# Values by 64x64 quarters, scores moved to the top of the tile, and conversions spread over three tiles

## The chip, the cores and the metric

One core of a Trainium2 chip runs one program. TensorE multiplies matrices from SBUF into PSUM, which has eight banks of 512 float32 columns on 128 partitions. VectorE (DVE), ScalarE (ACT) and GpSimd (POOL) work on the results, and SyncE (SP) issues nearly all DMAs. Each engine works through its own queue in order. The metric is the device time of one execution in microseconds (us). Before the change it is 1263.37 us, the median of three executions (1262.73 to 1265.43).

## The reference, cut to what matters

Attention inside chunks of 64 tokens (8 batches, 8 heads of 64 columns, 576 tokens each), then two feed-forward layers over all 4608 tokens:

```python
scores = scale * q_c @ k_c.T;  scores -= max(scores)      # per chunk of 64 tokens
attn = exp(scores) / (sum(exp(scores)) + 1e-9)
x = attn @ v_c                                            # heads side by side: 512 columns
h = x @ w_in                                              # 512 -> 1024
solu = h * softmax(h);  ln = (solu - mean) / sqrt(var + 1e-6) * g_ln
y = ln @ w_out                                            # 1024 -> 512
h2 = y @ w_in2                                            # 512 -> 2048
out = maximum(0.01 * h2, h2) @ w_out2                     # 2048 -> 512
```

Everything is float32 at the interface. The weights come as 64-bit words and are converted to float32 on the chip ("pieces" of 512 columns).

## The kernel before, in words

The first part of the program, about 550 us, takes the tokens in 36 tiles of 128: two chunks of 64 in every tile, eight heads in four pairs. For a tile it does, over several turns of the loop `for t in range(1, T + 2)`: scores (`qk_mm`), maxima, subtraction and exponentials (`softmax_a`), sums and division (`softmax_b`), transposition (`pt_mm`, `pt_copy`), values (`pv_mm`), splitting of the result into a high and a low part (`x_split`: `x_hi` on ACT, `x_lo` on DVE), the first layer in two halves of 512 columns (`ff1_mm(t, 0)` and `ff1_mm(t, 1)`, twelve matmuls each), softmax and normalisation (`solu_*`), transposition (`lnT_mm`, `lnT_split`), and, from tile 5 on, one group of the second matrix a turn (`y1_group`, 24 matmuls). The second part, the last 710 us, is the second feed-forward layer as a chain of matmuls (`h2_product`, `out_product`); the change does not touch it, except that its PSUM pool is opened later under another name.

The order on every engine is written out by hand: it is the order of the calls in the loop. In turn t the scores are those of a later tile: tile t + 2 at the top of the turn while t <= AHEAD = 5, and from t = 5 on tile t + 3, inside `attend(t)`, straight behind the values of tile t + 1. Two kinds of turn matter. In most, `y1_group` stands between `pt_mm(t + 1)` and `attend(t)`. In a "late" turn (t = 5, 9, 13, ... 33) `attend(t)` comes earlier, before `ff1_mm(t, 1)`, and `y1_group` stands at the end of the turn. "Tile t" below also means turn t.

Values before: V lies in `vbd` as block-diagonal operands with zeros, so that one matmul has 128 partitions of keys (two heads) and 64 output columns; 16 such matmuls make a tile. Their result lies in one bank, `ptx`, which `pt_mm` uses too; the scores have two banks, `s0` and `s1`. In tile 1 the scores are in the `ef` banks.

Conversion of a piece: ACT takes magnitudes (`take_magnitudes`, L101), DVE clamps and shifts (`convert_a`, L108 and L110) and joins the bits (`convert_b`, L114 and L118), POOL and ACT finish it. In turns 2, 3 and 5 all of this stands at the end of the turn, in later ones between `softmax_b` and the end.

Of the kernel before, what the change touches and what calls it, by code (L numbers as in the profile page):

```python
# [17 lines left out]
P = 128  # L18
# [34 lines left out]
def kernel(  # L53
# [18 lines left out]
    ps1 = ctx.enter_context(tc.tile_pool(name="ps1", bufs=1, space=bass.MemoryType.PSUM))  # L72

    ps2 = ws = yp = None

    def bank(tag, name):
        return (ps2 if tag == "ef" else ps1).tile([P, 512], F32, tag=tag, name=name)

# [227 lines left out]
    with tc.manual_schedule():  # L306

        with ExitStack() as phase:
            ps2 = phase.enter_context(
# [10 lines left out]
            vbd = [pa.tile([P, KD, 2, 2, D], F32, tag=f"vbd{i}", bufs=1, name=f"vbd{i}") for i in range(2)]  # L320
# [18 lines left out]
            def qk_mm(t):  # L339
                ps = s_ps[t] = [  # L340
                    bank("ef" if t == 1 else f"s{e}", "s_ps").rearrange("p (h n) -> p h n", h=H)[:, :KD]
                    for e in range(2)
                ]
# [12 lines left out]

            def softmax_a(t):
# [53 lines left out]
            def x_hi(t):  # L411
                x = xs[t] = pa.tile([P, 2, KD, P], F32R, tag="xs", name="xs")
                act.activation(x[:, 0], x_ps[t], AF.Copy)  # L413

            def x_lo(t):
                ps, x = x_ps.pop(t), xs[t]
                dve.tensor_tensor(x[:, 1], ps, x[:, 0].bitcast(F32), op=ALU.subtract)
# [82 lines left out]
            def lnT_mm(t):  # L500
                u = us.pop(t)
                for hf in range(2):
                    tag = ("s0", "ptx")[hf] if t == T - 2 else "ef"
                    ps = ln_ps[t, hf] = bank(tag, "ln_ps").rearrange("p (i n) -> p i n", i=4)
# [19 lines left out]
            def y1_group(b, m):  # L524
                pairs = (slice(0, 2), slice(0, 3, 2), slice(1, 3))[b % 3]
                bnk = bank("s1" if (b, m) == (NB - 1, 0) else "ef", "y_ps")
# [50 lines left out]
            for i, eng in enumerate((dve, pool)):  # L577
                eng.memset(vbd[i][0:D, :, :, 1], 0.0)
                eng.memset(vbd[i][D:P, :, :, 0], 0.0)
# [20 lines left out]
            def exponentials(t):  # L600
                ps, sm = s_ps.pop(t), st8[t]
                for h in range(H):
                    act.activation(
                        es[t][:, h],
                        ps[h % 2][:, h // 2],
# [6 lines left out]
            def maxima(t):  # L612
                sm = st8[t] = pa.tile([P, 2, H], F32, tag="st8", name="st8")
                es[t] = pa.tile([P, H, D], F32, tag="es", name="es")
                for i in range(2):
                    dve.reduce_max(sm[:, 0, i::2], s_ps[t][i], axis=AX)
# [104 lines left out]
            for t in range(1, T + 2):  # L721
# [12 lines left out]
                if t <= AHEAD:  # L734
                    load_qk(t + 3)
# [13 lines left out]
                pieces = 0 if t in (1, 4) or t >= T - 2 else 2 if t in DOUBLE else 1  # L749
                if 0 < t <= AHEAD:  # L750
# [6 lines left out]
                if t <= AHEAD:  # L757
# [24 lines left out]
                if 1 < t < T:  # L782
                    solu_max(t, 0)
                if 1 <= t <= T:
# [22 lines left out]
                else:  # L807
# [28 lines left out]

        wb = ctx.enter_context(tc.tile_pool(name="wb", bufs=1, reuse_waits="tile"))
# [290 lines left out]
```

## Time and profile before

| | before |
|---|---|
| median of 3 executions | 1263.37 us |
| the profiled execution, device time | 1262.47 us |
| its span, first to last instruction | 1260.7 us |
| TensorE busy | 1228.4 us (97%) |
| DVE busy | 897.1 us (71%) |
| ACT busy | 573.3 us (45%) |
| POOL busy | 285.2 us (23%) |
| mean granted TensorE clock | 0.996 of full |

The device time is 1.8 us longer than the span. In a timeline row the first number is the start, the second the time from the first start to the last end of the merged instructions; ends of matmuls are modelled and overlap the next row, so what a step takes on TensorE is best read as the distance from its start to the start of the next row. A bracket at the end of a row is the idle time of the engine before it and what ended that. An fp32 matmul of 64 columns is recorded as two instructions, so a tile's 16 matmuls appear as x32.

### The profile page before, as it was taken

What the parts mean: (1) busy time and instruction counts of PE and PEld (TensorE: products, weight loads), DVE (VectorE), ACT (ScalarE), POOL (GpSimd) and SP (SyncE); (2) the same over time, 40 slices, a digit from 0 to 9 for tenths busy, and PEclk for the clock granted to TensorE, in tenths of its full rate; (3) what the DMA queues carried; (4) which work ended last, traced back from release to release, by engine and by line L of the source; (5) the groups of instructions that cost most, each with busy time, mean ns of one, the idle gap of its engine ahead of it and who ended that gap; (6) DMA issues with size and microseconds to landing.
All of it is one profiled execution on the core that took longest, in us unless ns stands there. A gap on an engine that the chain in (4) does not pass through costs nothing.

```text
span 1260.7 us, 22964 instructions
## 1 busy us (share of the span) xinstructions
PE 1228.4 (97%) x8554; PEld 1092.5 (87%) x8554; DVE 897.1 (71%) x1603; ACT 573.3 (45%) x1078; POOL 285.2 (23%) x390
## 2 busy tenths in 40 slices
PE   5989999999999999999999999999999999999998
PEld 4678888778878887899989988998999899989987
DVE  7888778877886887435786677577657766775674
ACT  6645545555545545433442353344235243442451
POOL 0355656655765666200000000000000000000000
PEclk8999999999999999999999999999999999999999
DMA  7535546645676573549889978988898899789676
GB/s 247 163 96 149 176 151 216 235 161 160 207 210 198 157 224 107 186 170 322 262 293 306 293 242 274 310 269 247 291 309 255 262 297 302 240 260 301 197 221 197
DMA packets 171070, 288.83 MB, mean 229 GB/s; under 512 B 50000, under 2 KB 80720, under 8 KB 169936
## 3 DMA queue, kind: packets, MB, share of 16 engines
q1 hardware_dynamic: 170592, 286.78, 71.4%
q8 instruction: 69, 1.13, 0.4%
q10 hardware_dynamic: 368, 0.59, 0.1%
q14 instruction: 41, 0.34, 0.1%
HBM read 239.08 MB, written 48.23 MB: 228 GB/s over the span
## 4 chain that ended last, share of the span: by engine, by line
PE 85%; DVE 8%; ACT 4%; DMA 1%; issue 1%; SPq 0%; ACTq 0%
PE h_ps L871 28%; PE o_ps L928 19%; PE y_ps L534 13%; PE h_ps L435 10%; PE o_ps L939 10%; PE x_ps L399 2%; PE ln_ps L507 2%; PE s_ps L349 1%; DVE lnT L522 1%; ACT us L458 1%; PE pt_ps L383 1%; DVE us L466 1%; DVE wf L114 1%; DVE wf L118 1%; DVE wf L108 1%
## 5 line engine op out<-in xcount | busy, mean ns | idle before, releaser
L871 PE MATMUL h_ps<-yo,w_s 128*128 128x384 f32 x2016 | 351.0, 334 | 0.0
L871 PEld LDWEIGHTS h_ps<-yo,w_s 128*128 128x128 f32 x2016 | 349.3, 188 | 0.7
L928 PE MATMUL o_ps<-wo_s,yo 128*128 128x512 f32 (+1 forms) x1016 | 262.9, 393 | 0.0
L435 PE MATMUL h_ps<-wi,xs 128*128 128x512 f32 x864 | 211.2, 397 | 1.0 <-ACT xs L413 0.7
L534 PE MATMUL y_ps<-lnT,wo 128*128 128x512 f32 (+1 forms) x888 | 204.2, 386 | 0.0
L928 PEld LDWEIGHTS o_ps<-wo_s,yo 128*128 128x128 f32 x1016 | 179.0, 188 | 28.7
L435 PEld LDWEIGHTS h_ps<-wi,xs 128*128 128x128 f32 x864 | 159.7, 189 | 35.3 <-ACT xs L413 0.8
L534 PEld LDWEIGHTS y_ps<-lnT,wo 128*128 128x128 f32 x888 | 161.7, 188 | 31.9
L939 PEld LDWEIGHTS o_ps<-wo_s,yo 128*128 128x128 f32 x1008 | 144.7, 188 | 15.6
L271 DVE TENSOR_TENSOR yo<-c,yo 128x768 fp32r<-128x768 f32 x144 | 132.4, 951 | 32.0 <-ACT yo L270 30.6
L939 PE MATMUL o_ps<-wo_s,yo 128*128 128x256 f32 x1008 | 149.7, 283 | 0.0
L850 ACT ACTIVATE c<-h_c 128x384 f32<-128x384 f32 x144 | 72.9, 526 | 127.4 <-DVE h_c L882 127.4
L882 DVE TENSOR_TENSOR h_u<-h_ps,h_p 128x384 f32<-128x384 f32 x96 | 53.3, 555 | 106.3 <-PE h_ps L871 99.6
L270 ACT ACTIVATE yo<-c 128x768 fp32r<-128x768 f32 x144 | 113.1, 838 | 7.1 <-DVE c L912 5.5
L466 DVE SCALAR_TENSOR_TENSOR us<-h_ps,us 128x512 f32<-128x512 f32 x72 | 48.7, 690 | 35.4 <-ACT us L458 35.3
L373 POOL TENSOR_TENSOR es<-es,st 128x512 f32<-128x512 f32 x33 | 34.6, 1049 | 156.2 <-DVE st L372 100.7
L522 DVE TENSOR_TENSOR lnT<-ln_ps,lnT 128x512 fp32r<-128x512 f32 x72 | 45.8, 679 | 33.7 <-ACT lnT L518 33.7
L458 ACT ACTIVATE us<-h_ps,z 128x512 f32<-128x512 f32 x72 | 48.7, 682 | 40.2 <-DVE z L454 40.2
L270 ACT ACTIVATE yo<-a 128x768 fp32r<-128x768 f32 x36 | 30.0, 840 | 72.6 <-DVE a L265 72.6
L882 DVE TENSOR_TENSOR h_c<-h_ps,h_u 128x384 f32<-128x384 f32 x96 | 53.2, 554 | 12.9 <-PE h_ps L871 12.3
L366 ACT ACTIVATE es<-es 128x512 f32<-128x512 f32 x33 | 20.8, 632 | 89.4 <-DVE es L365 89.4
L399 PEld LDWEIGHTS x_ps<-pt,vbd 128*64 128x64 f32 x1152 | 37.4, 140 | 26.7 <-ACT pt L389 18.4
(90 smaller groups left out, 1426.7 us busy)
## 6 DMA issues: line engine op xcount, KB each, us to landing
w_s<-wi_d SPq DMA_DIRECT2D x336, 256.0 KB, 4.1
wo_s<-wo_d SPq DMA_DIRECT2D x168, 512.0 KB, 4.6
wi_d<-wi SPq DMA_DIRECT2D x8, 1792.0 KB, 6.3
wo_d<-wi SPq DMA_DIRECT2D x8, 1792.0 KB, 7.0
raw<-in_w_out SPq DMA_DIRECT2D x24, 512.0 KB, 5.1
raw<-in_w_in SPq DMA_DIRECT2D x23, 512.0 KB, 5.2
vbd<-in_v SPq DMA_DIRECT2D x72, 128.0 KB, 5.1
a<-y_d SPq DMA_DIRECT2D x24, 384.0 KB, 5.3
```

Of the source, the lines that this page charges most:

```text
L270: act.activation(o[:, 0], x, AF.Copy)
L271: dve.tensor_tensor(o[:, 1], x, o[:, 0].bitcast(F32), op=ALU.subtract)
L399: pe.matmul(ps[e * D : (e + 1) * D, i, c * D : (c + 1) * D], lhsT=vv[:, i, c, e], rhs=pp[:, i, c * D : (c + 1) * D], start=True, stop=True,)
L435: pe.matmul(hs[t, n], lhsT=x[:, a, kk, :], rhs=w[:, b, kk % 2, n, :], start=(kk == 0 and a == 0 and b == 0), stop=(kk == KD - 1 and a == 1),)
L458: act.activation(u[:, c], hs[t, n], AF.Exp, bias=z[:, 0:1], accum_out=z[:, 8 + n : 9 + n])
L466: dve.scalar_tensor_tensor(u[:, c], hs.pop((t, n)), 1.0 / FF1, u[:, c], op0=ALU.mult, op1=ALU.mult, accum_out=z[:, 10 + n : 11 + n],)
L534: pe.matmul(ps[:, part], lhsT=w[:, a, kk % 4, m * P : (m + 1) * P], rhs=lnT[:, c, kk, pairs, :][:, part], start=(kk == 0 and a == 0 and c ...
L850: act.activation(blocks[block, j // 2][:, j % 2], src, AF.Prelu, alpha=0.01)
L871: pe.matmul(ps, lhsT=w[:, a, kk * P : (kk + 1) * P], rhs=y[:, c, kk, :], start=(first and kk == 0 and a == 0 and c == 0), stop=(kk == 1 an ...
L882: dve.tensor_tensor(o, ps, x, op=ALU.add)
L928: pe.matmul(ps[:, : 2 * P * (a.stop - a.start)], lhsT=x[:, 0, kk, m * P : (m + 1) * P], rhs=w[:, kk, a].rearrange("p a n -> p (a n)"), sta ...
L939: pe.matmul(sums[p % 2][m][:, : 2 * P], lhsT=x[:, 1, kk, m * P : (m + 1) * P], rhs=w[:, kk, 0], start=False, stop=(i == PAIRS - 1 and kk = ...
```

## The change

1. Values by quarters: V is loaded without zeros (`vs`, four DMAs for a tile in place of two, in runs of 512 bytes in place of 256), and each matmul has 64 partitions of keys, 64 output columns and 64 columns of probabilities. There are 16 a tile as before. Heads that share the upper or lower partitions write to different banks, so a tile's values need two banks; they are the two of the scores, now one PSUM tile `s`. In tile 1 the values take both `ef` banks, and `x_split` has two instructions on each engine there. The four memsets of zeros at the start go.
2. The subtraction, the maxima and `x_split` go over both banks with one instruction each; the heads lie in another order inside a tile.
3. Scores: `qk_mm(t + 2)` and `softmax_a(t + 2)` stand at the top of the turn in all turns; `attend` keeps the values and their split.
4. In late turns `attend(t)` stands behind `ff1_mm(t, 1)`.
5. First conversions: magnitudes at the end of turns 1 and 2, `convert_a` in the middle of turn 2 and at the end of turn 3, `convert_b` in the middle of turns 3 and 4.

```diff
             def load_v(t):
...
-                for e in range(2):
-                    r = slice(e * D, (e + 1) * D)
-                    sync.dma_start(out=vbd[t % 2][r, :, :, e], in_=v[t, r])
+                for r in range(2):
+                    for e in range(2):
+                        sync.dma_start(
+                            out=vs[t % 2][r * D : (r + 1) * D, 2 * e : 2 * e + 2],
+                            in_=v[t, e * D : (e + 1) * D, r::2],
+                        )
...
             def softmax_a(t):
...
-                for i in range(2):
-                    dve.reduce_max(sm[:, 0, i::2], ps[i], axis=AX)
-                for i in range(2):
-                    m = sm[:, 0, i::2].unsqueeze(2).to_broadcast([P, KD, D])
-                    dve.tensor_tensor(e[:, i::2], ps[i], m, op=ALU.subtract)
+                top = sm[:, 0].rearrange("p (e i) -> p e i", e=2)
+                dve.reduce_max(top, ps, axis=AX)
+                dve.tensor_tensor(
+                    e.rearrange("p (e i) n -> p e i n", e=2),
+                    ps,
+                    top.unsqueeze(3).to_broadcast([P, 2, KD, D]),
+                    op=ALU.subtract,
+                )
...
             def pv_mm(t):
-                ps = x_ps[t] = bank("ptx", "x_ps").rearrange("p (i n) -> p i n", i=KD)
-                vv, pp = vbd[t % 2], pt.pop(t)
-                for i in range(KD):
+                if t == 1:
+                    ps = [bank("ef", "x_ps") for r in range(2)]
+                    ps = [x.rearrange("p (a n) -> p a n", a=KD)[:, :2] for x in ps]
+                    x_ps[t] = [(r, x) for r, x in enumerate(ps)]
+                else:
+                    both = two_banks("x_ps").rearrange("p r (a n) -> p r a n", a=KD)[:, :, :2]
+                    ps = [both[:, r] for r in range(2)]
+                    x_ps[t] = [(slice(0, 2), both)]
+                vv, pp = vs[t % 2], pt.pop(t)
+                for a in range(2):
                     for c in range(2):
-                        for e in range(2):
-                            pe.matmul(
-                                ps[e * D : (e + 1) * D, i, c * D : (c + 1) * D],
-                                lhsT=vv[:, i, c, e],
-                                rhs=pp[:, i, c * D : (c + 1) * D],
-                                start=True,
-                                stop=True,
-                            )
+                        for r in range(2):
+                            k = slice(r * D, (r + 1) * D)
+                            for e in range(2):
+                                pe.matmul(
+                                    ps[r][e * D : (e + 1) * D, a, c * D : (c + 1) * D],
+                                    lhsT=vv[k, 2 * e + a, c],
+                                    rhs=pp[k, 2 * e + a, c * D : (c + 1) * D],
+                                    start=True,
+                                    stop=True,
+                                )
...
             def attend(t):
 
                 pv_mm(t + 1)
-                if AHEAD <= t < T - 3:
-                    qk_mm(t + 3)
-                    load_qk(t + 4)
                 x_split(t + 1)
-                if AHEAD <= t < T - 3:
-                    softmax_a(t + 3)
...
-                if 0 < t <= AHEAD:
+                if t + 2 < T:
                     qk_mm(t + 2)
...
-                if t <= AHEAD:
+                if t + 2 < T:
                     softmax_a(t + 2)
...
+                if t == 2:
+                    convert_a()
+                elif 2 < t < AHEAD:
+                    convert_b(load=False)
+                    owed = 1
...
-                    elif t < T - 1:
+                    elif t < T - 1 and not late:
                         attend(t)
                     if 1 < t < T:
                         ff1_mm(t, 1)
+                    if late and 1 < t < T - 1:
+                        attend(t)
...
-                        take_magnitudes(pieces)
-                        convert_a(pieces)
-                        convert_b(pieces, load=t == AHEAD)
-                        owed = pieces if t < AHEAD else 0
+                        take_magnitudes(pieces if t == AHEAD else t < 3)
+                        convert_a(pieces if t == AHEAD else t == 3)
+                        if t == AHEAD:
+                            convert_b(pieces)
```

TensorE, from the values of tile 7 (`x_ps`) to the transposition of tile 8 (`pt_ps`); `s_ps` are scores, `ln_ps` a transposition, `h_ps` the first layer. Before:

```order
L399 MATMUL x_ps<-pt,vbd_105 64x64 x16
L349 MATMUL s_ps<-kb_103,qt 64x64 x16
L507 MATMUL ln_ps<-ident,us 128x128 x8
L435 MATMUL h_ps<-wi_173,xs 128x512 x4
L435 MATMUL h_ps<-wi_355,xs 128x512 x4
L435 MATMUL h_ps<-wi_173,xs 128x512 x2
L435 MATMUL h_ps<-wi_355,xs 128x512 x2
L435 MATMUL h_ps<-wi_173,xs 128x512 x4
L435 MATMUL h_ps<-wi_355,xs 128x512 x4
L435 MATMUL h_ps<-wi_173,xs 128x512 x2
L435 MATMUL h_ps<-wi_355,xs 128x512 x2
L383 MATMUL pt_ps<-ident,es 128x128 x4
```

And now, at the same place:

```order
L421 MATMUL x_ps<-pt,vs_105 64x64 x16
L535 MATMUL ln_ps<-ident,us 128x128 x8
L460 MATMUL h_ps<-wi_172,xs 128x512 x4
L460 MATMUL h_ps<-wi_353,xs 128x512 x4
L460 MATMUL h_ps<-wi_172,xs 128x512 x2
L460 MATMUL h_ps<-wi_353,xs 128x512 x2
L359 MATMUL s_ps<-kb_103,qt 64x64 x16
L460 MATMUL h_ps<-wi_172,xs 128x512 x4
L460 MATMUL h_ps<-wi_353,xs 128x512 x4
L460 MATMUL h_ps<-wi_172,xs 128x512 x2
L460 MATMUL h_ps<-wi_353,xs 128x512 x2
L396 MATMUL pt_ps<-ident,es 128x128 x4
```

The scores moved from behind the values to between the two halves of the first layer.

DVE, from the maximum of tile 2's first half (L450) to the start of turn 3 (L454); `xs` is `x_lo`, `lnT` the split behind the transposition, `wf` a piece. Before:

```order
L450 TENSOR_REDUCE z<-h_ps 128x1
L417 TENSOR_TENSOR xs<-x_ps,xs 128x512
L522 TENSOR_TENSOR lnT<-ln_ps,lnT 128x4x128 x2
L108 TENSOR_SCALAR wf<-wf 128x512
L110 TENSOR_SCALAR wf<-wf 128x512
L114 SCALAR_TENSOR_TENSOR wf<-raw,wf 128x512
L118 SCALAR_TENSOR_TENSOR wf<-raw,wf 128x512
L450 TENSOR_REDUCE z<-h_ps 128x1
L454 TENSOR_TENSOR z<-z 128x1
```

And now:

```order
L475 TENSOR_REDUCE z<-h_ps 128x1
L110 TENSOR_SCALAR wf<-wf 128x512
L112 TENSOR_SCALAR wf<-wf 128x512
L442 TENSOR_TENSOR xs<-x_ps,xs 128x2x2x128
L550 TENSOR_TENSOR lnT<-ln_ps,lnT 128x4x128 x2
L475 TENSOR_REDUCE z<-h_ps 128x1
L479 TENSOR_TENSOR z<-z 128x1
```

The first two steps of the piece moved ahead of `x_lo`, the other two out of this turn.

TensorE at the start of the program, the first layer of tile 1 behind its values, with what each row waits for. Before:

```order
L399 MATMUL x_ps<-pt,vbd_105 64x64 x14
L435 MATMUL h_ps<-wi_173,xs 128x512 [waits Activation_49]
L435 MATMUL h_ps<-wi_173,xs 128x512 x7
L435 MATMUL h_ps<-wi_173,xs 128x512 [waits DVE_49]
L435 MATMUL h_ps<-wi_173,xs 128x512 x3
```

And now:

```order
L421 MATMUL x_ps<-pt,vs_105 64x64 x12
L460 MATMUL h_ps<-wi_172,xs 128x512 [waits Activation_49]
L460 MATMUL h_ps<-wi_172,xs 128x512 [waits DVE_49]
L460 MATMUL h_ps<-wi_172,xs 128x512 x2
L460 MATMUL h_ps<-wi_172,xs 128x512 [waits Activation_49]
L460 MATMUL h_ps<-wi_172,xs 128x512 x5
L460 MATMUL h_ps<-wi_172,xs 128x512 [waits DVE_49]
```

The wait for DVE that stood at the ninth matmul now stands at the second, because that one writes the `ef` bank that held tile 1's values.

## Rows read from the trace of the kernel before

**Rows 1.** The page: span, TensorE's busy time, the costliest group and its idle time.
```profile
span 1260.7 us, 22964 instructions
PE 1228.4 (97%) x8554; PEld 1092.5 (87%) x8554; DVE 897.1 (71%) x1603; ACT 573.3 (45%) x1078; POOL 285.2 (23%) x390
...
L871 PE MATMUL h_ps<-yo,w_s 128*128 128x384 f32 x2016 | 351.0, 334 | 0.0
```
**Rows 2.** Waits of TensorE: line, what for, us in total, times, longest.
```profile
PE x_ps L399 <- ACT pt L389: 14.0, 12, 3.5
```
**Rows 3.** Timeline of TensorE, tile 14 into tile 15, no waits.
```profile
212.87 1.15 PE L399 MATMUL x_ps<-pt,vbd 128*64 128x64 f32 x32
213.95 0.69 PE L349 MATMUL s_ps<-kb,qt 64*64 64x64 f32 x32
214.58 1.09 PE L507 MATMUL ln_ps<-ident,us 128*128 128x128 f32 x8
215.43 5.74 PE L435 MATMUL h_ps<-wi,xs 128*128 128x512 f32 x24
221.00 0.60 PE L383 MATMUL pt_ps<-ident,es 128*128 128x128 f32 x4
221.36 5.71 PE L534 MATMUL y_ps<-lnT,wo 128*128 128x512 f32 x24
227.00 1.15 PE L399 MATMUL x_ps<-pt,vbd 128*64 128x64 f32 x32
```
**Rows 4.** Timeline of TensorE, tile 2, scores at the top of the turn.
```profile
44.10 3.02 PE L435 MATMUL h_ps<-wi,xs 128*128 128x512 f32 x12
46.95 0.60 PE L383 MATMUL pt_ps<-ident,es 128*128 128x128 f32 x4
...
49.44 3.01 PE L435 MATMUL h_ps<-wi,xs 128*128 128x512 f32 x12
52.38 0.69 PE L349 MATMUL s_ps<-kb,qt 64*64 64x64 f32 x32
```
**Rows 5.** Timeline of TensorE, values in late tile 17 and what follows.
```profile
253.31 1.25 PE L399 MATMUL x_ps<-pt,vbd 128*64 128x64 f32 x32 [2.10 <-ACT pt L389]
...
255.55 3.99 PE L435 MATMUL h_ps<-wi,xs 128*128 128x512 f32 x12
```
**Rows 6.** Stretches: from:to, length, TensorE busy (instructions), granted clock, DMA share, GB/s.
```profile
253.00:259.00 6.00, 5.69 (x75) 0.72 0.02 4
```
**Rows 7.** Timeline of TensorE, values in turns 1, 3 and 4.
```profile
40.80 1.15 PE L399 MATMUL x_ps<-pt,vbd 128*64 128x64 f32 x32 [0.61 <-ACT pt L389]
...
59.01 1.15 PE L399 MATMUL x_ps<-pt,vbd 128*64 128x64 f32 x32 [1.67 <-ACT pt L389]
...
71.53 1.15 PE L399 MATMUL x_ps<-pt,vbd 128*64 128x64 f32 x32 [3.54 <-ACT pt L389]
```
**Rows 8.** Timeline of DVE, end of tile 3: the conversion and the maximum behind it.
```profile
63.79 1.18 DVE L108 TENSOR_SCALAR wf<-wf 128x512 f32<-128x512 f32 x1
...
66.44 0.69 DVE L114 SCALAR_TENSOR_TENSOR wf<-raw,wf 128x512 uint32<-128x512 uint32 x1
...
67.78 0.68 DVE L450 TENSOR_REDUCE z<-h_ps 128x1 f32<-128x512 f32 x1
```
**Rows 9.** Timeline of TensorE, start of the program, first layer of tiles 1 and 0.
```profile
30.15 2.11 PE L435 MATMUL h_ps<-wi,xs 128*128 128x512 f32 x8 [0.69 <-ACT xs L413]
32.53 3.96 PE L435 MATMUL h_ps<-wi,xs 128*128 128x512 f32 x16 [0.27 <-DVE xs L417]
36.42 0.69 PE L349 MATMUL s_ps<-kb,qt 64*64 64x64 f32 x32
```
**Rows 10.** Timeline of DVE: x_lo at the start, in tile 14 and in tile 16.
```profile
31.79 0.68 DVE L417 TENSOR_TENSOR xs<-x_ps,xs 128x512 fp32r<-128x512 f32 x1
...
214.73 0.69 DVE L417 TENSOR_TENSOR xs<-x_ps,xs 128x512 fp32r<-128x512 f32 x1 [1.09 <-ACT xs L413]
...
246.03 0.68 DVE L417 TENSOR_TENSOR xs<-x_ps,xs 128x512 fp32r<-128x512 f32 x1
```

More of the change, by code (lines that the diff above doesn't have):

```diff
@@ L71, with two_banks @@
     dram = ctx.enter_context(tc.tile_pool(name="dram", bufs=1, space=bass.MemoryType.DRAM))
-    ps1 = ctx.enter_context(tc.tile_pool(name="ps1", bufs=1, space=bass.MemoryType.PSUM))
-    ps2 = ws = yp = None
+    ps1 = ps2 = ws = yp = None
     def bank(tag, name):
         return (ps2 if tag == "ef" else ps1).tile([P, 512], F32, tag=tag, name=name)
+    def two_banks(name):
+        return ps1.tile([P, 2, 512], F32, tag="s", name=name)
     ident = const.tile([P, P], F32, name="ident")
@@ L308 @@
         with ExitStack() as phase:
+            ps1 = phase.enter_context(
+                tc.tile_pool(name="ps1", bufs=1, space=bass.MemoryType.PSUM)
+            )
             ps2 = phase.enter_context(
@@ L318 @@
             kbs = [pa.tile([P, KD, 2, D], F32, tag=f"kb{i}", bufs=1, name=f"kb{i}") for i in range(2)]
-            vbd = [pa.tile([P, KD, 2, 2, D], F32, tag=f"vbd{i}", bufs=1, name=f"vbd{i}") for i in range(2)]
+            vs = [pa.tile([P, KD, 2, D], F32, tag=f"vs{i}", bufs=1, name=f"vs{i}") for i in range(2)]
             qt, es, pt, xs, hs, us, st8 = {}, {}, {}, {}, {}, {}, {}
@@ L332, in load_v @@
                     return
-                for e in range(2):
-                    r = slice(e * D, (e + 1) * D)
-                    sync.dma_start(out=vbd[t % 2][r, :, :, e], in_=v[t, r])
+                for r in range(2):
[4 more added lines that the diff above has]
+                        )
             s_ps = {}
             def qk_mm(t):
[L340 to L343, printed above, removed]
+                if t == 1:
+                    ps = [bank("ef", "s_ps") for e in range(2)]
+                    s_ps[t] = ps = [x.rearrange("p (h n) -> p h n", h=H)[:, :KD] for x in ps]
+                else:
+                    both = two_banks("s_ps").rearrange("p e (h n) -> p e h n", h=H)[:, :, :KD]
+                    s_ps[t], ps = both, [both[:, e] for e in range(2)]
                 kb, qq = kbs[t % 2], qt.pop(t)
@@ L412, in x_hi @@
                 x = xs[t] = pa.tile([P, 2, KD, P], F32R, tag="xs", name="xs")
-                act.activation(x[:, 0], x_ps[t], AF.Copy)
+                hi = x[:, 0].rearrange("p (a r) n -> p r a n", a=2)
+                for r, ps in x_ps[t]:
+                    act.activation(hi[:, r], ps, AF.Copy)
             def x_lo(t):
-                ps, x = x_ps.pop(t), xs[t]
-                dve.tensor_tensor(x[:, 1], ps, x[:, 0].bitcast(F32), op=ALU.subtract)
+                hi, lo = (xs[t][:, e].rearrange("p (a r) n -> p r a n", a=2) for e in range(2))
+                for r, ps in x_ps.pop(t):
+                    dve.tensor_tensor(lo[:, r], ps, hi[:, r].bitcast(F32), op=ALU.subtract)
             def ff1_mm(t, half, ks=None):
@@ L502, in lnT_mm @@
                 for hf in range(2):
-                    tag = ("s0", "ptx")[hf] if t == T - 2 else "ef"
-                    ps = ln_ps[t, hf] = bank(tag, "ln_ps").rearrange("p (i n) -> p i n", i=4)
+                    if t == T - 2 and hf == 0:
+                        bnk = two_banks("ln_ps")[:, 0]
+                    else:
+                        bnk = bank("ptx" if t == T - 2 else "ef", "ln_ps")
+                    ps = ln_ps[t, hf] = bnk.rearrange("p (i n) -> p i n", i=4)
                     for i in range(4):
@@ L525, in y1_group @@
                 pairs = (slice(0, 2), slice(0, 3, 2), slice(1, 3))[b % 3]
-                bnk = bank("s1" if (b, m) == (NB - 1, 0) else "ef", "y_ps")
+                bnk = two_banks("y_ps")[:, 1] if (b, m) == (NB - 1, 0) else bank("ef", "y_ps")
                 ps = bnk.rearrange("p (a n) -> p a n", a=2)
@@ L614, in maxima @@
                 es[t] = pa.tile([P, H, D], F32, tag="es", name="es")
-                for i in range(2):
-                    dve.reduce_max(sm[:, 0, i::2], s_ps[t][i], axis=AX)
+                for e in range(2):
+                    ps = s_ps[t][e] if t == 1 else s_ps[t][:, e]
+                    dve.reduce_max(sm[:, 0, e * KD : (e + 1) * KD], ps, axis=AX)
                 dve.tensor_scalar_mul(sm[:, 0, :], sm[:, 0, :], -scale)
@@ L748 @@
                 late = g == 0 or t == T - 1
-                pieces = 0 if t in (1, 4) or t >= T - 2 else 2 if t in DOUBLE else 1
-                if 0 < t <= AHEAD:
+                pieces = 0 if t < AHEAD or t >= T - 2 else 2 if t in DOUBLE else 1
+                if t + 2 < T:
                     qk_mm(t + 2)
@@ L832 @@
                         y1_group(*bm)
+        ps1 = ctx.enter_context(
+            tc.tile_pool(name="ps1b", bufs=1, space=bass.MemoryType.PSUM, reuse_waits="tile")
+        )
         wb = ctx.enter_context(tc.tile_pool(name="wb", bufs=1, reuse_waits="tile"))
```

12 lines of the change are left out of this document (6 added, 6 removed).

## The prediction

> **What bounds the kernel now.** I read the page first, then the waits of TensorE, then its timeline over whole tiles, and DVE's timeline where TensorE waits. TensorE is busy 1228.4 of 1260.7 us, and the costliest group of the second part has no idle time before it [rows 1]. So the second part, which the change leaves alone, gives nothing. In the first part a tile is a chain of TensorE steps each of which begins where the last ends [rows 3]: what a step costs there costs the program that much. The one wait that recurs is that of the values for the copy of the transposed probabilities (`pt_copy`, ACT): 14.0 us in 12 waits [rows 2]. The reader is to see two sources of a gain, shorter steps and these waits, and ask of everything else whether it can push TensorE back.
>
> **The values by quarters.** A tile's values take from 212.87 to 213.95, 1.08 us, the scores behind them to 214.58, 0.63 us [rows 3]. Both are 32 recorded instructions; the scores' are 64x64 with 64 columns, which is the new form of the values, in the same alternation of partitions, columns and banks. So I price the new values at 0.63: 0.45 less a tile. The bounds are 1.08 (a quarter gains nothing) and 0.63; no row has anything shorter.
>
> **The scores' new place.** This is the edit that works against the gain. Before, a turn has values, scores and transposition in a row, then 24 matmuls of the first layer without a break, 215.43 to 221.00, 5.57 us [rows 3]. Now the scores stand between the two halves. Tile 2 shows both halves in that place: the one ahead of scores 2.94 us (49.44 to 52.38), the one behind scores 2.85 us (44.10 to 46.95) [rows 4], 5.79 together, 0.22 more than 5.57. A turn with `y1_group` takes 14.13 us now (212.87 to 227.00) [rows 3]. Afterwards: scores 0.63, first half 2.85, transposition 0.36, `y1_group` 5.64, values 0.63, transposition 0.85, second half 2.94, together 13.90. So 0.23 of the 0.45 is left.
>
> A rule of the Trainium skill speaks here (page TensorEngine Tiling (Array Packing), section Tiling Modes): switching the tiling mode drains TensorE. The trace agrees in direction with the 0.22 us above; by the rule a turn had three switches and now has four, and without a drain the turn would be 13.68 and the sum 1236, which is the first rival below.
>
> Late turns have the same steps and I give them the same 0.23. Turn 5 loses the second of its two score blocks and turn 33 gains one, which cancels. From turn 5 to turn 33 that is 29 x 0.23 = 6.7 us. Turns 1 to 4 have the scores at the top already and keep the whole 0.45: 1.8. Turn 34 computes no scores: 0.45. Sum 8.9 us; I take 8.7, since in turn 1 part of it meets the delay below. Bounds: 0 if a quarter costs 1.08 and the scores' place costs nothing, 15.7 if only the first holds its promise (35 x 0.45); a loss of 6.4 (29 x 0.22) if a quarter gains nothing and the place costs.
>
> **The waits in steady turns.** From turn 6 on nine of the 12 waits, 0.3 to 2.1 us, come to 8.2: the 14.0 of [rows 2] less 0.61, 1.67 and 3.54 in turns 1, 3 and 4 [rows 7]. The largest stand in late turns, where the values come soon after the transposition: 2.10 in turn 17 [rows 5]. There the values now come one half of the first layer later, 2.94 us, which is more than any of these waits. The clock goes with it: behind the wait of turn 17 the granted clock is 0.72 over six microseconds [rows 6], so part of the stretch ran at 1.2 GHz in place of 2.4, and half of the first layer took 3.99 in place of 3.01 [rows 4, 5], 1.0 us more. Together 9.2. A few of the 0.3 us waits may stay: 0.6. Gain 8.6; bounds 4 and 9.2.
>
> What is late next is the scores at the top of a turn, which now must find the shared banks read by `x_lo` of the tile before. In tile 14 `x_lo` begins 0.78 us after the values end by start-to-start (213.95 to 214.73) and lasts 0.69; the second half of the first layer would then still run for over two microseconds. In tile 16, where DVE is behind, it ends at 246.71, hardly before that half does [rows 10]. But DVE's work up to `x_lo` is the same as before: `softmax_a` moved from behind the previous tile's `x_lo` to ahead of this one's. And `x_lo` no longer has ACT's exponential, waiting for DVE, between itself and the split of `lnT`. I count nothing; bound 0.5 in each of the 14 or so turns where DVE is behind, 7 us. Queued behind a waiting score block is all of TensorE's turn, so such a wait would count in full. The values' wait for `softmax_a` has the first half, transposition and `y1_group`, almost 9 us, as cover.
>
> The one-instruction maxima and subtractions save DVE start costs only; DVE is not the bound, so nothing. The two extra DMAs a tile lie on SP, which has a turn's lead for them; nothing.
>
> **The first conversions.** The values of tiles 4 and 5 wait 1.67 and 3.54 us for `pt_copy` [rows 7]; that copy is behind the exponentials of the layer, these behind a maximum on DVE, and that behind a whole conversion, 63.79 to 67.78, 3.99 us in turn 3 [rows 8]. Now turn 2 ends without any of it, so its 1.67 goes. Turn 3 ends with two of the four instructions, which took 2.65 of the 3.99 beside POOL's work (63.79 to 66.44), so at least 1.34 goes, and what goes earlier in the turn goes too: I take 2.2 of 3.54. The other halves stand in mid-turn where DVE waits for ACT; they may hold `x_lo` and with it the scores for 0.3. Gain 3.6; bounds 0 and 5.2.
>
> **The start.** Here the change adds a wait. Before, eight matmuls of tile 1's first layer ran (30.15 to 32.26) while DVE came to `x_lo`; the other 16 began at 32.53 [rows 9]. Now the second matmul writes the bank that held the values and must wait for the first of the two `x_lo` instructions. `x_lo` began at 31.79 and took 0.68 [rows 10]; half of it ends at about 32.2. Then 23 matmuls remain, at 0.24 each (3.89 us by 16), 5.6 us: scores at 37.8 in place of 36.42. Behind this wait are tile 0's layer, its maxima on DVE and ACT's exponentials; `pt_copy` and the values of tile 2 follow them. In turn 1 TensorE waits 0.61 before the values [rows 7], which it had to spare, so I book 0.8 of the 1.4 as a loss; bounds 0 and 1.4. The memsets that go stood in an idle DVE: nothing. Four DMAs for V in place of two push later loads back in SP's queue, with the same bytes in fewer pieces: nothing, bound 1 us either way. At the end of the first part a group of `y1_group` shares banks with a transposition and waits at most for one DVE subtraction, 0.69 [rows 10]: nothing.
>
> **The sum.** 8.7 + 8.6 + 3.6 - 0.8 = 20.1 us. The profiled execution took 1262.5 (its span and 1.8 around it), 0.9 less than the median of 1263.4. 1262.5 - 20.1 = 1242.4; with the median as base 1243.3. I say 1243.
>
> **The rivals.**
> The scores' place is free: the turn keeps all 0.45, 6.4 us more, 1236 to 1237. For it: ends of matmuls are modelled, and the 0.22 compares different turns. Against it: tile 2 shows it on both sides of the scores.
> Shared banks: where DVE is behind, the scores wait for `x_lo`, 7 us as bounded above: 1250. For it: 246.71 in tile 16 is only just in time, and turns get shorter while DVE's work does not. Against it: DVE also loses waits.
> The quarters do not run beside each other as the scores' do and values stay at 1.08: 1243 + 35 x 0.45 = 1259. Against it: the same form runs at 0.63.
> Slower: shared banks in every turn, a mechanism of its own. Values, ACT copy, DVE subtraction and the next scores are now one loop through one pair of banks. If DVE reached `x_lo` so late in all 29 turns that the scores waited over 0.8 us each, 23 us, the gain would be gone; at 1 us each the time is 1272. That needs `x_lo` over 3 us later than in tile 14 in every turn. Beside it stands the skill's rule (the same page, section Performance Considerations) that tiling speeds up TensorE but not the evacuation of PSUM; DVE's 71% [rows 1] does not bear it out here.
>
> **How the numbers follow.** Forecast, 1238 to 1248: 0.60. Place free, 1236: 0.12. Shared banks in some turns, 1250: 0.16. Quarters gain nothing, 1259: 0.05. Slower, 1272: 0.04. Something between that I have not named, about no change: 0.03. The range 1234 to 1253 holds the first three. A measurement of this kernel cannot tell 0.2%, 2.5 us, from no change. Faster by more: 0.93; within: 0.03; slower: 0.04.
>
> **What would show it.** Values of 0.6 to 0.7 us from their start to the next row; scores between two halves of 2.85 to 2.95; a turn of 13.9 us; no wait of the values for `pt_copy` over 0.5 us from turn 6 on, no stretch of clock 0.72; the values of tile 4 without a wait and those of tile 5 with 1 to 1.5; the scores of tile 3 a microsecond later. I would be wrong if `s_ps` shows waits for DVE `xs` of several microseconds in sum, or if values stay over 0.8 us.

## The result, and the profile after

| | before | after |
|---|---|---|
| median (6 executions each, side by side) | 1264.09 us | 1241.94 us |
| lowest to highest | 1262.73 to 1265.43 | 1241.21 to 1242.75 |
| profiled execution | 1262.47 us | 1242.7 us |

The ratio is 0.9825, 95% interval 0.9812 to 0.9837. The forecast was 1243.0 (1234 to 1253). The profiled execution of before is 1.6 us below its median and that of after 0.8 above its own, so the medians lie 22.2 us apart and the spans 19.8. Two lines of the page of after, against [rows 1]: the span, and the busy time of the engines.

```profile
span 1240.9 us, 22946 instructions
...
PE 1218.2 (98%) x8554; PEld 1073.5 (87%) x8554; DVE 892.8 (72%) x1536; ACT 572.0 (46%) x1079; POOL 285.9 (23%) x388
```

TensorE has 10.2 us less work and 9.6 us fewer gaps. Its waits after (line, what for, us in total, times, longest):

```profile
PE x_ps L421 <- ACT pt L402: 2.6, 2, 1.4
PE h_ps L460 <- DVE xs L442: 2.3, 1, 2.3
...
PE s_ps L359 <- DVE xs L442: 1.2, 2, 0.8
```

The values' 14.0 us in 12 waits [rows 2] are 2.6 in two, both in the start: 1.36 at 27.81, which before had too (1.44 at 28.31, listed as `issue` and not among the 14.0), and 1.23 in turn 1, where before had 0.61 [rows 7]. Two waits on `x_lo` (DVE `xs`) are new or larger. TensorE's timeline of after, in order of time: the start, the values in turn 1, the scores behind the values of tile 5, the transposes of turn 7, a steady turn, a late turn, the beginning of the second part.

```profile
31.84 8.36 PE L460 MATMUL h_ps<-wi,xs 128*128 128x512 f32 x23 [2.33 <-DVE xs L442]
40.13 0.69 PE L359 MATMUL s_ps<-kb,qt 64*64 64x64 f32 x32
...
44.03 0.69 PE L421 MATMUL x_ps<-pt,vs 64*64 64x64 f32 x32 [1.23 <-ACT pt L402]
...
73.43 0.69 PE L359 MATMUL s_ps<-kb,qt 64*64 64x64 f32 x32 [0.75 <-DVE xs L442]
...
104.79 0.60 PE L396 MATMUL pt_ps<-ident,es 128*128 128x128 f32 x4
...
208.27 0.69 PE L421 MATMUL x_ps<-pt,vs 64*64 64x64 f32 x32
208.90 1.09 PE L535 MATMUL ln_ps<-ident,us 128*128 128x128 f32 x8
209.75 3.01 PE L460 MATMUL h_ps<-wi,xs 128*128 128x512 f32 x12
212.69 0.69 PE L359 MATMUL s_ps<-kb,qt 64*64 64x64 f32 x32
213.31 3.02 PE L460 MATMUL h_ps<-wi,xs 128*128 128x512 f32 x12
216.17 0.60 PE L396 MATMUL pt_ps<-ident,es 128*128 128x128 f32 x4
...
222.19 0.69 PE L421 MATMUL x_ps<-pt,vs 64*64 64x64 f32 x32
...
244.00 0.60 PE L396 MATMUL pt_ps<-ident,es 128*128 128x128 f32 x4
...
257.95 0.60 PE L396 MATMUL pt_ps<-ident,es 128*128 128x128 f32 x4
...
531.82 58.41 PE L902 MATMUL h_ps<-yo,w_s 128*128 128x384 f32 x336
```

The rows of before that answer to the last four places, from its timeline of TensorE, with the scores of late tile 17 among them:

```profile
107.39 0.60 PE L383 MATMUL pt_ps<-ident,es 128*128 128x128 f32 x4
...
249.59 0.60 PE L383 MATMUL pt_ps<-ident,es 128*128 128x128 f32 x4
...
254.49 1.13 PE L349 MATMUL s_ps<-kb,qt 64*64 64x64 f32 x32
...
267.61 0.60 PE L383 MATMUL pt_ps<-ident,es 128*128 128x128 f32 x4
...
551.54 48.70 PE L871 MATMUL h_ps<-yo,w_s 128*128 128x384 f32 x280
```

Values take 0.63 us (208.27 to 208.90) against 1.08 [rows 3], a steady turn 13.92 (208.27 to 222.19) against 14.13, the late turn of tile 17 13.95 (244.00 to 257.95) against 18.02 (249.59 to 267.61). From turn 7's transposes to the second part it is 427.03 us against 444.15, 17.1 less. Up to turn 7 only 2.6 were gained, because the scores of tile 3 begin 3.7 us later, 40.13 against 36.42 [rows 9]; from those scores to turn 7 it is 64.66 against 70.97, 6.3 less. Together 19.7, as the spans say (19.8).

### The profile page after: what moved, and what is told of

It is laid out like the page before. It is cut to its first block, busy times and chain, and to the rows that moved or that the text cites. A ratio compares the mean times of both kernels' runs of the same rounds, so it can differ in the third digit from the quotient of the medians.

```text
span 1240.9 us, 22946 instructions
## 1 busy us (share of the span) xinstructions
PE 1218.2 (98%) x8554; PEld 1073.5 (87%) x8554; DVE 892.8 (72%) x1536; ACT 572.0 (46%) x1079; POOL 285.9 (23%) x388
## 4 chain that ended last, share of the span: by engine, by line
PE 94%; DVE 4%; ACT 1%; DMA 0%; POOL 0%; issue 0%; POOLq 0%
PE h_ps L902 28%; PE o_ps L959 19%; PE y_ps L562 16%; PE h_ps L460 15%; PE o_ps L970 10%; PE ln_ps L535 2%; PE x_ps L421 2%; PE s_ps L359 1%; PE pt_ps L396 1%; DVE wf L116 1%; DVE wf L120 0%; DVE us L491 0%; DVE z L475 0%; DMA raw<-in_w_in 0%; DVE wf L112 0%; DVE wf L110 0%
## 5 line engine op out<-in xcount | busy, mean ns | idle before, releaser
L460 PE MATMUL h_ps<-wi,xs 128*128 128x512 f32 x864 | 219.9, 404 | 3.5 <-DVE xs L442 2.3
L475 DVE TENSOR_REDUCE z<-h_ps 128x1 f32<-128x512 f32 x72 | 48.9, 681 | 19.7 <-PE h_ps L460 19.6
L570 ACT ACTIVATE ys<-y_ps 128x512 f32<-128x512 f32 x36 | 21.4, 593 | 87.6 <-PE y_ps L562 86.5
L881 ACT ACTIVATE c<-h_ps 128x384 f32<-128x384 f32 x48 | 23.6, 492 | 76.2 <-PE h_ps L902 76.2
```

The lines of the kernel that those rows point to most:

```text
L460: pe.matmul(hs[t, n], lhsT=x[:, a, kk, :], rhs=w[:, b, kk % 2, n, :], start=(kk == 0 and a == 0 and b == 0), stop=(kk == KD - 1 and a == 1),)
L475: dve.reduce_max(sol[t][:, 8 + n : 9 + n], hs[t, n], axis=AX, negate=True)
L881: act.activation(blocks[block, j // 2][:, j % 2], src, AF.Prelu, alpha=0.01)
```

## The experiments

All times are medians of four or five executions; intervals are of the ratio to the kernel before on the same chip. "After" is 1241.94 throughout. The first four experiments share a chip, the others ran on three more. The median of before beside them lies between 1264.1 and 1265.3 us, so a difference between kernels of different chips is good to about 1 us.

### The banks of the start

```diff
-    ps = [bank("ef", "x_ps") for r in range(2)]
+    ps = [bank(tag, "x_ps") for tag in ("ef", "ptx")]
```

> The values of tile 1 go to one bank of ef and to ptx, in place of two banks of ef, so that the second matmul of ff1 of tile 1 finds a bank that held no values. Theory A (the wait for x_lo at the start, and the clock that falls with it, is the term that the prediction booked too small): the wait of 2.33 us at 31.84 goes, ff1 of tile 1 starts some 2 us earlier and runs at the full clock, scores of tile 3 at 36.5 to 37.5 in place of 40.13, and the time falls by 2.5 to 3.5 us against the changed kernel, to 1238.5 to 1239.5. Theory B (the start is hidden by a transfer, the keys and queries of tile 3, or given back within turns 2 to 5): scores of tile 3 move, but the time stays within 0.7 us of 1241.9.

1239.03 us, 0.980 (0.9786 to 0.9813): 2.9 less than after. Its timeline at the same place:

```profile
29.08 2.11 PE L460 MATMUL h_ps<-wi,xs 128*128 128x512 f32 x8 [0.42 <-ACT xs L437]
...
35.76 0.69 PE L359 MATMUL s_ps<-kb,qt 64*64 64x64 f32 x32
```

Eight matmuls run ahead of `x_lo` again, as in [rows 9], and the scores come 4.4 us earlier. The spans differ by 3.8 (1237.1 against 1240.9), the medians by 2.9. Theory A holds; nothing hides the start. This is the fastest kernel of the study.

### Work ahead of the wait

```diff
     high(7)
+    warm(24)
     ff1_mm(1, 0)
```

> 24 transposes of the identity into a spare bank stand ahead of the first ff1 of tile 1: the wait for x_lo stays where it is, TensorE only has work in front of it. Theory A1 (most of the 3.7 us is the granted clock, which falls to 0.50 from 32 to 36 us): the clock stays near 1 from 32 to 41, scores of tile 3 come 2 to 3 us earlier, and the time falls by 2 to 3 us. Theory A2 (the wait itself is the loss, 2.3 us of idle engine): the clock may be better, but scores of tile 3 come at most 1 us earlier and the time stays within 1 us of 1241.9; the transposes could even add a part of their 24 x 0.06 = 1.4 us.

1239.96 us, 0.9807 (0.9794 to 0.9820): 2.0 less. Its timeline, and then the stretch of the clock (from:to, length, TensorE busy, granted clock, DMA share, GB/s), ahead of that of after:

```profile
28.41 2.84 PE L655 MATMUL spare<-ident 128*128 128x128 f32 x24
31.40 5.92 PE L460 MATMUL h_ps<-wi,xs 128*128 128x512 f32 x24
37.25 0.69 PE L359 MATMUL s_ps<-kb,qt 64*64 64x64 f32 x32
```
```profile
32.00:36.00 4.00, 4.00 (x18) 1.00 0.70 211
```
```profile
29.00:32.00 3.00, 0.66 (x2) 0.86 0.28 79
32.00:36.00 4.00, 4.00 (x10) 0.50 0.87 265
```

The first layer still cannot pass `x_lo`: its 24 matmuls start at 31.40, and of those of after one stands ahead of the wait and 23 start at 31.84. But they run at the full clock, and the scores come at 37.25, which is 0.8 us behind before. So of the 3.7 us that the profiled execution of after loses at this place the wait is 0.8 and the lower clock 2.9: in after TensorE was busy 0.66 us in three, and then 1.2 GHz (0.50 of full) was granted for the whole of the next four. By the medians the transposes, 0.12 us each where 0.06 was expected, give back 2.0. The Trainium skill (page TensorE: Matmul & The Clock Gate, Part 1) says that the granted clock follows how busy the engine has been; this pair of runs agrees.

### The values as they were

```diff
...
+                both = bank("ptx", "x_ps").rearrange("p (a r n) -> p r a n", a=2, r=2)
...
-                                    lhsT=vv[k, 2 * e + a, c],
-                                    rhs=pp[k, 2 * e + a, c * D : (c + 1) * D],
+                                    lhsT=vv[:, 2 * e + a, c, r],
+                                    rhs=pp[:, 2 * e + a, c * D : (c + 1) * D],
...
```

The values lie in bank `ptx` again, which the scores do not share, and the memsets of zeros are back.

> The changed kernel's order with the values as they were: 128 partitions deep with half of the weights zero, 32 matmuls of 64 columns one after the other into bank ptx. Theory A (the quarters are worth 0.45 us in each tile, and the waits that went were removed by the order alone): values take 1.08 us in place of 0.63, turns 14.36 in place of 13.91, no waits of values come back, 34 x 0.45 = +15.3 us, less 2.5 to 3.5 at the start (no wait there for a bank), so about +12 us, 1253 to 1255. Theory B (the shorter values only let TensorE wait less elsewhere, or the quarters' shared banks cost as much as they save): within 4 us of 1241.9.

1252.88 us, 0.991 (0.9896 to 0.9923), 13.9 above the kernel with the start's banks mended, which is the fair partner, since neither has the long wait in the start. Its timeline:

```profile
217.32 5.73 PE L557 MATMUL y_ps<-lnT,wo 128*128 128x512 f32 x24
222.98 1.15 PE L416 MATMUL x_ps<-pt,vs 128*64 128x64 f32 x32
224.06 1.09 PE L530 MATMUL ln_ps<-ident,us 128*128 128x128 f32 x8
...
231.70 0.47 PE L557 MATMUL y_ps<-lnT,wo 128*128 128x512 f32 x1
```

Values 1.08, turns 14.38 (217.32 to 231.70), 0.46 above 13.92: the quarters are worth their full 0.45 in a steady turn, and no wait comes back with the long values. Theory A. The sum is 13.9 and not 35 x 0.45 = 15.8: from turn 4's transposes to turn 5's the mended kernel, whose scores wait 0.70 for `x_lo` in a shared bank there, takes 9.66 us (63.44 to 73.10) against 8.92 (64.24 to 73.16), so 1.2 of the gain is lost at that place.

### The first conversions where they were

```diff
-                pieces = 0 if t < AHEAD or t >= T - 2 else 2 if t in DOUBLE else 1
+                pieces = 0 if t in (1, 4) or t >= T - 2 else 2 if t in DOUBLE else 1
...
-                if t == 2:
-                    convert_a()
-                elif 2 < t < AHEAD:
-                    convert_b(load=False)
-                    owed = 1
...
```

> The changed kernel with the first conversions of w_out1 where they were: a piece each at the end of turns 2 and 3 and none in steps. Theory A (the conversions hold up the values of tiles 4 and 5 on VectorE): waits of values of 1 to 3.5 us in turns 3 and 4 come back, +1.7 to +5 us, 1243.6 to 1247. Theory B (with the scores at the tile's top the early turns are held by something else, and the move is worth nothing): within 1 us of 1241.9.

1248.97 us (1246.39 to 1249.06), 0.9873 (0.986 to 0.9887): 4.5 to 7.1 above after, more than the prediction's 3.6 and mostly more than expected here. Its timeline:

```profile
61.97 0.69 PE L421 MATMUL x_ps<-pt,vs 64*64 64x64 f32 x32 [2.10 <-ACT pt L402]
...
74.49 1.02 PE L421 MATMUL x_ps<-pt,vs 64*64 64x64 f32 x32 [3.84 <-ACT pt L402]
75.44 4.25 PE L460 MATMUL h_ps<-wi,xs 128*128 128x512 f32 x12
```

Both waits of [rows 7] return, a little longer, and behind the second one half of the first layer takes 4.25 in place of 3.02 (granted clock 0.74 from 76 to 80). Theory A.

### The scores behind the values

```diff
                 pv_mm(t + 1)
+                if AHEAD <= t < T - 3:
+                    qk_mm(t + 3)
+                    load_qk(t + 4)
                 x_split(t + 1)
+                if AHEAD <= t < T - 3:
+                    softmax_a(t + 3)
...
```

> The changed kernel with the scores and their softmax behind the values again from turn 5 on, as before the change, in the banks that values and scores now share. Theory A (the shared banks are why the scores had to move: they wait for x_hi and x_lo of the values ahead of them): in the changed kernel values end at 208.90 and x_lo ends at 210.44, so the scores wait some 1.5 us in each of 27 turns, or 0.7 with lnT between them, less the 0.22 that their place between two matmuls of ff1 costs now: +13 to +35 us, 1255 to 1277. Theory B (a slow TensorE is given the time back in the next turn, since nothing else bounds it): TensorE has no slack in a turn, so this would show as turns of 13.91 us still and a time within 3 us of 1241.9.

1306.99 us, 1.0332 (1.0316 to 1.0348), slower than before. Its waits, and the scores behind the values in turns 14 and 15 on TensorE:

```profile
PE s_ps L359 <- DVE xs L442: 55.3, 30, 3.6
```
```profile
227.25 0.69 PE L359 MATMUL s_ps<-kb,qt 64*64 64x64 f32 x32 [1.52 <-DVE xs L442]
...
244.62 1.13 PE L359 MATMUL s_ps<-kb,qt 64*64 64x64 f32 x32 [3.64 <-DVE xs L442]
```

Theory A in its mechanism, with almost twice its upper price: most steady turns wait 1.52 us, most late ones 1.77, and turns 15, 23 and 31, the second of two turns that convert two pieces each, 3.6. Behind the first of these three the granted clock is 0.50 from 244 to 248. So with shared banks the move of the scores is a condition of the quarters. The loop that the prediction made its slower rival exists; the scores' place keeps clear of it.

### What removed the waits for pt_copy

Three kernels. In the first, which keeps the quarters, the changed kernel has late turns' values back ahead of `ff1_mm(t, 1)`; the other two are the kernel with the values as they were (1252.88), with the scores behind the values, without and with that edit.

> The changed kernel with the values of the late turns (every fourth) ahead of the second half of ff1 again. Theory A (their later place is what removed the waits for pt_copy from turn 6 on): 8 late turns wait 1 us each again, +8 us, 1250, with waits of x_ps for pt_copy in the late turns. Theory B (the waits went with the scores: in the old order ScalarE had the exponentials of the scores ahead of pt_copy, in the new one pt_copy runs 0.25 us behind the transposes, from 244.69 to 245.29, while lnT ends at 245.23): 0.1 to 0.3 us a turn, 1242 to 1244.

> The kernel with the values as they were (1252.9; bank ptx, so the scores share no bank with them) and with the scores behind the values again from turn 5 on; the late turns' values stay behind the second half of ff1. Theory A (the scores' new place costs 0.22 us a turn and removes no wait that the late turns' order doesn't remove too): 27 x 0.22 = -6 us, 1247, with no waits of values from turn 6 on. Theory B (the scores at the tile's top are what gives ScalarE and VectorE their time): waits of values for pt_copy come back, some of 8 us, 1250 to 1256.

> As the kernel beside it, and the late turns' values ahead of the second half of ff1 again: the order of before from turn 6 on, with only the start and the conversions of the changed kernel. Theory A (the order of before makes the 8.2 us of waits and 1.0 of clock, and either of the two moves removes them): +9 us against the kernel beside it, some 1256, waits of x_ps for pt_copy of 2 us in late turns. Theory B (the waits went with the start or the conversions, which are no longer late): within 1.5 us of the kernel beside it.

They measured 1241.88 us (0.9814, 0.9801 to 0.9827), 1257.01 (0.9936, 0.9923 to 0.9950) and 1259.58 (1256.35 to 1259.88; 0.995, 0.9937 to 0.9962). The values' waits for `pt_copy` are in the first those of after, 2.6 us in two, and in the second 1.5 in four. A wait of the second, then one of the third:

```profile
PE h_ps L455 <- DVE us L486: 5.0, 3, 1.7
```
```profile
PE x_ps L416 <- ACT pt L402: 8.8, 10, 2.1
```

The first shows that beside the scores' move the late values' place is worth nothing: theory B. The second shows that without the scores' move it only turns the wait of the values into one of the first layer for its bank (`h_ps` for DVE `us`). Neither theory foresaw that wait: the time is 4 us above the kernel with the scores at the top where A said 6 below, so A is out, and B's waits came, but at another step. The third has again what before had, 8.2 us from turn 6 on and 0.6 in turn 1 [rows 2, 7], but its step over the second, 2.6 us with overlapping ranges, doesn't settle a price. So the scores' move, of which the prediction asked only what it costs, is enough to remove the waits, and the late place is not. Its mechanism is in the timelines of late tile 17, DVE and then ACT, before and after:

```profile
247.29 0.74 DVE L365 TENSOR_TENSOR es<-s_ps,st 128x256 f32<-128x256 f32 x2
249.21 1.29 DVE L522 TENSOR_TENSOR lnT<-ln_ps,lnT 128x512 fp32r<-128x512 f32 x2 [1.18 <-ACT lnT L518]
250.42 0.68 DVE L450 TENSOR_REDUCE z<-h_ps 128x1 f32<-128x512 f32 x1
...
252.66 0.59 ACT L389 ACTIVATE pt<-pt_ps 128x512 f32<-128x512 f32 x1
```
```profile
238.18 1.28 DVE L550 TENSOR_TENSOR lnT<-ln_ps,lnT 128x512 fp32r<-128x512 f32 x2
240.62 0.69 DVE L475 TENSOR_REDUCE z<-h_ps 128x1 f32<-128x512 f32 x1 [1.17 <-PE h_ps L460]
...
241.42 0.68 DVE L372 TENSOR_REDUCE st<-s_ps 128x8 f32<-128x512 f32 x1
...
244.69 0.60 ACT L402 ACTIVATE pt<-pt_ps 128x512 f32<-128x512 f32 x1 [1.19 <-PE pt_ps L396]
```

Before, the softmax of the scores stood ahead of the layer's maximum (250.42), and so did a wait of 1.18 us for ACT's part of `lnT`, which is queued behind the scores' exponential (248.06). The maximum came 0.8 us behind the transposes at 249.59, and the exponentials and `pt_copy` (252.66) behind it. Now the maximum (240.62) comes first, waits only for TensorE, and stands 3.4 us ahead of the transposes at 244.00; the softmax fills DVE's time while ACT is at the exponentials, and `pt_copy` (244.69) waits only for the transposes. Two kernels that differ in nothing but the scores' place show the same step in this turn, the second of the three and the one with the values as they were:

```profile
246.91 0.68 DVE L470 TENSOR_REDUCE z<-h_ps 128x1 f32<-128x512 f32 x1
```
```profile
242.34 0.69 DVE L470 TENSOR_REDUCE z<-h_ps 128x1 f32<-128x512 f32 x1 [1.24 <-PE h_ps L455]
```

With the scores behind the values the maximum is 0.8 us behind its transposes (246.07), with the scores at the top 3.4 ahead of them (245.72).

The order alone does not make the long waits. Before, the values wait 2.10 us in turns 17, 25 and 33 (253.31, 371.05 and 487.43), and at most 0.33 in the other turns from 6 on. Turns 14 and 15, 22 and 23, 30 and 31 ahead of these convert two pieces each, which points at a DVE that is behind from the conversions; but turn 9, as far behind turns 5 to 7 with two pieces each, has no wait, and no run takes the doubled conversions away, so this is not shown.

### The scores beside the transposes

```diff
...
                 if 1 <= t <= T:
                     solu_b(t - 1)
+                if AHEAD < t < T - 2:
+                    qk_mm(t + 2)
+                    softmax_a(t + 2)
                 if t + 1 < T:
                     pt_mm(t + 1)
```

> The banks of the start as in the first experiment (1239.0), and from turn 6 on the scores stand directly ahead of the transposes of the probabilities, behind all 24 matmuls of ff1, and no longer between its halves. Theory A (each passage between 64x64 scores and 512-column matmuls costs 0.07 to 0.15 us, as 2.94 + 2.85 us against 5.57 says, and scores beside transposes save them): 28 turns of 13.7 in place of 13.91, -6 us, 1233. Theory B (the passage costs the same beside transposes, or the softmax that starts 2.9 us later makes values wait for pt_copy): 1238 to 1242, or slower with waits of x_ps for ScalarE.

> The scores beside the transposes as in the run before (1254.7, with 10.2 us of values waiting for pt_copy), but pt_copy is issued on ScalarE straight behind its transposes, ahead of the conversions' magnitudes and of the exponentials of the new scores. Theory A (the loss there was only the order on ScalarE; a turn of TensorE alone is 13.80 there, values 0.62 + lnT 0.85 + ff1 5.66 + scores 0.62 + transposes 0.41 + y1 5.64, against 13.91): waits of values go, 28 x 0.11 = -3 us against 1239.0, so 1236. Theory B (the softmax of the scores and with it the solu functions and the conversions come later in every turn, and the wait only moves, to lnT or to h_ps): 1240 to 1255.

> As the kernel beside it, but with the scores behind the transposes of the probabilities, between these and the matmuls of y1. Theory A (a passage between 64x64 tiles and 512-column matmuls costs some 0.1 us each way, wherever it is): one such passage, and one from transposes, are left here as there, within 1 us of the kernel beside it. Theory B (it is the passage into the scores from 512-column matmuls that costs, 0.15 of the 0.22 us; from the transposes it costs less): 0.1 us a turn, -3 us against the kernel beside it.

All three contain the mended start (1239.03) and are slower than it: 1254.72 us (0.9916, 0.9902 to 0.9929), 1249.23 (0.9878, 0.9861 to 0.9896) and 1252.23 (0.9902, 0.9887 to 0.9918). Waits and TensorE's timeline of the first, then DVE's of the second:

```profile
PE x_ps L421 <- ACT pt L402: 10.2, 8, 1.8
```
```profile
222.32 5.73 PE L460 MATMUL h_ps<-wi,xs 128*128 128x512 f32 x24
227.98 0.69 PE L359 MATMUL s_ps<-kb,qt 64*64 64x64 f32 x32
```
```profile
232.22 0.69 DVE L491 SCALAR_TENSOR_TENSOR us<-h_ps,us 128x512 f32<-128x512 f32 x1 [1.06 <-ACT us L483]
...
233.95 0.68 DVE L372 TENSOR_REDUCE st<-s_ps 128x8 f32<-128x512 f32 x1
```

The whole first layer takes 5.66 us here (222.32 to 227.98) against 2.94 + 2.86 around the scores, and a turn without a wait 13.80 (171.74 to 185.54) against 13.92: the new place's price is real, and about half of it, 0.12, can be had back, as theory A of the second says. But the place costs far more elsewhere. The waits of the first run from turn 6 on stand in turns 15, 16, 23, 24, 31 and 32, the second turn with two pieces to convert and the one behind it, which are steady turns in after; these six alone lose 15.2 us over 13.80. The softmax leaves the gap in which DVE waits for ACT (now idle, 1.06) and comes behind it, so the conversions, the exponentials and `pt_copy` are late there; with `pt_copy` put first the wait moves to the transposition of `lnT` (`ln_ps` for ACT `ys`, 5.5 us in six). Theory B in the first two. The third, 3 us above the second, speaks against its theory B, and its turns without a wait take 13.89 (157.45 to 171.34); it differs in waits too, so a passage's price can't be read from the totals.

## Why the prediction was right, and which of its terms were not

| step | predicted | measured |
|---|---|---|
| values by quarters, a tile | 0.45 | 0.45 (0.63 us); 13.9 in sum by undoing it, against the mended start |
| scores between the halves | 0.22 lost | 0.23: 2.94 + 2.86 against 5.57 [rows 3] |
| a steady turn | 13.90 | 13.92 |
| turn 7 to the second part | 6.4 + 0.45 + 8.6 = 15.5 | 17.1 |
| first conversions | 3.6 | 4.1 between the timelines; 4.5 to 7.1 by undoing it |
| the start | 0.8 lost | 3.7 later in the profiled execution; 2.9 by undoing it |
| sum | 20.1 | 19.8 between the spans, 22.2 between the medians |

**Steady turns.** The price of a quarter and of the scores' place held to some 0.01 us, each from a row of the same form in a comparable place. The Trainium skill's rule (page TensorEngine Tiling (Array Packing), section Tiling Modes) that a switch of mode drains TensorE agrees with the 0.23. The run with the scores beside the transposes makes as many switches and saves about half of it, so the price hangs on the neighbours too. The first rival, a free place, is false.

**The waits from turn 6 on.** Right in effect, wrong in its cause: "There the values now come one half of the first layer later" is not what removed them, as the first of those three kernels showed. The scores' move did, through DVE's order. The prediction had the edge in hand ("no longer has ACT's exponential, waiting for DVE, between itself and the split of `lnT`") and used it only to dismiss a rival. That the gain came out near its size is luck: the waits were counted as gone, whichever edit removed them. The size was low: 28 turns at 0.21 and the 0.45 of turn 34 leave about 10.8 of the 17.1 for waits, against 8.6. The late turn of tile 17 alone lost 3.9 us over a steady one, where 2.10 + 1.0 were booked: the scores from 254.49 to 255.55 [rows 5] were slow as well, 1.06 against 0.63. The clock had to be counted over all rows of the slow stretch, not over one. Nor does it fall behind every such wait. Around the same wait in turn 33 the granted clock stayed at 1.00 in before (486 to 492, TensorE busy 4.57 us), and was 0.72 in the third kernel of the waits (481 to 487, busy 4.46).

**The conversions.** The values of tile 5 have no wait in the list, where 1 to 1.5 was forecast; and the scores behind them wait 0.75 for `x_lo`, where 0.3 was. From turn 3's transposes to turn 5's after takes 18.19 us (58.73 to 76.92) against 23.18 (55.87 to 79.05); without the 0.45 of two tiles' values that is 4.1 where 3.6 was booked. Undone alone the edit costs more than the waits of before were: 2.10 and 3.84 against 1.67 and 3.54 [rows 7], and 1.2 of clock.

**The start.** This is the step that was mis-sized: "scores at 37.8 in place of 36.42". The wait is there and would give 37.25 at full clock; the step priced the 23 matmuls at 0.24 each and did not ask what an idle TensorE does to the granted clock, though [rows 6] showed it in another place. 2.9 of the 3.7 us are that. Nor was there anything to spare in turn 1: its wait of 0.61 became 1.23 (44.03), and what came back was 0.5, from the scores of tile 3 to those values: 3.90 (40.13 to 44.03) in place of 4.38 (36.42 to 40.80). The start cancelled by luck against the two terms that were too small, so the sum came out closer than its terms.

**The rivals.** Waits of the scores for `x_lo` are 1.2 us in two places, none in a steady turn. The values as they were, 1252.88, and the scores behind, 1306.99, show that the third and fourth rival were far off for this kernel, and the fourth is real one edit away.

What stays open: the third kernel of the waits and before share their order from turn 6 on and have the same nine waits, and yet take 447.1 (101.49 to 548.62) and 444.2 us from turn 7 to the second part. 1.5 of the difference stand in turn 33 (17.42 against 15.89), behind whose wait the clock fell in one of the two only, as shown above, and 0.5 in a wait for a load; the last 0.9 has no cause here. Whether the 3.5 us between that kernel's executions come from the clock is not shown.

## What to carry to other kernels

Before a wait of the busiest engine is put down to the place of the waiting step, look at what stands ahead of its releaser on the other engines: moving the scores helped by what it cleared on DVE, and the visible move next to the wait was worth nothing. Where a new wait falls into a stretch with little work around it, price the work behind it at the lower clock too, as an upper bound, and look for a bank that avoids the wait. A sum that comes out right says little of its terms; undoing each edit alone does.

## What the runs showed of the hardware

A wait of 2.3 us in a stretch of three with 0.66 us of work was followed by four at a granted clock of 0.50; 24 transposes without a use (2.84 us) in the same place kept it at 1.00 and paid for themselves with 2.0 us of the total. Waits of 2.10 us in before were followed by a granted clock of 0.72 over six microseconds in turn 17 [rows 6] and of 1.00 in turns 25 (369 to 375) and 33 (486 to 492) of the same execution. A 64x64 quarter matmul with 64 columns cost what the prediction read from the scores, 32 recorded instructions in 0.63 us, against 1.08 for 128 partitions deep, although the useful products are the same.
